# Reordering the queues of a fused attention and gated-unit block: value weights ahead of four tiles of x, fewer filler matmuls

## The chip, the cores and the metric

The kernel runs on one core of a Trainium2 chip (the seven other cores have nothing to do). The metric is the device time of one execution in microseconds, as the median of some runs; lower is better. Four engines compute: TensorE (PE in the profile, with PEld for its weight loads), VectorE (DVE), ScalarE (ACT) and GpSimd (POOL). SyncE (SP) computes nothing; it issues nearly all DMA transfers. Each engine works through its own queue in order and waits on semaphores for what others produce.

## The reference

One layer on x of 2048 rows by 448 columns, in bf16, with 16 heads of 28 columns. Both halves start with a layer norm.

```python
    def _A_ref(x, wqkv, w_phi, wo):
        ...
        pq = jnp.einsum("bhsd,hdf->bhsf", q, w_phi)
        pk = jnp.einsum("bhsd,hdf->bhsf", k, w_phi)
        phi_q = jnp.concatenate([_softmax(pq, axis=-1), _softmax(-pq, axis=-1)], axis=-1)
        phi_k = jnp.concatenate([_softmax(pk, axis=-1), _softmax(-pk, axis=-1)], axis=-1)
        kv = jnp.einsum("bhsf,bhsd->bhfd", phi_k, v)
        z  = jnp.einsum("bhsf->bhf", phi_k)
        num = jnp.einsum("bhqf,bhfd->bhqd", phi_q, kv)
        den = jnp.einsum("bhqf,bhf->bhq", phi_q, z)[..., None] + 1e-6
        o = num / den
        return (lambda x, *d: x.transpose(*d))(o, 0, 2, 1, 3).reshape(B, S, D) @ wo

    def _B_ref(x, w_gate, w_up, w_down):
        g = jnp.einsum("bsd,df->bsf", x, w_gate)
        u = jnp.einsum("bsd,df->bsf", x, w_up)
        h = _sigmoid(g) * u
        return jnp.einsum("bsf,fd->bsd", h, w_down)

    h = x + _A_ref(_layernorm(x, axis=-1), A_wqkv, A_w_phi, A_wo)
    h2 = h + _B_ref(_layernorm(h, axis=-1), B_w_gate, B_w_up, B_w_down)
```

## The kernel before

**Tiles and stages.** The 2048 rows are 16 tiles of 128, numbered 0 to 15. The kernel is one straight program without loops on the chip. Its stages run into each other:

- Front (0 to about 17 us). Weights for keys (ld_k0, ld_k2) and values (ld_v0, ld_v2) and x (x0, x1, x2, x4, ..., the later ones two tiles each, so x6 holds tiles 6 and 7) are loaded. DVE takes the mean and variance of each tile (bst, agg, lines 557 and 558), POOL the inverse root (pow1, line 566), and xn is the normalised tile. Tiles 0 to 3 are transposed on PE (xT0 to xT3, copied out by xT0e to xT3e, lines 550 and 543), tiles 4 to 15 by DMA transposes that SP issues (line 595). The key weights are folded with w_phi on PE (wT, w2m0, copied out by w2e0, line 634), so that the key features come from one product; the query weights likewise (w2m1, w2e1). Filler matmuls on zeros (warm0 to warm9, line 536) stand where PE would have nothing to do.
- Key features (about 10 to 43 us). For tiles 0 to 3, ppa/ppb are the key products of two tiles and vva/vvb the value products; from tile 4 on, pva/pvb do both for one tile. ACT takes the two exponentials of each tile (ek, lines 673 and 674) and copies the values (v1, line 543); DVE sums (ss, line 677) and inverts (rs, line 683); POOL or DVE multiplies (phi, line 687); PE accumulates phi times v into banks 6 and 7 (kva/kvb, line 697), started by a small constant product (seed, line 711). PE squeezes the query products (pqa/pqb, exponentials eq on ACT, line 725) in between.
- Attention output (about 43 to 57 us). The sums in banks 6 and 7 are masked into kvz (kvzA to kvzD, lines 754 and 758). For each tile num is the product with the query features, and DVE does rsm, qq, b, c and rden (lines 802 to 810); o is the normalised output, oT its transpose. The output projection of tiles 0 and 1 (wof0, wof1) includes x, so bs2 and ag2 take the second layer norm's statistics from PSUM, h0 and h1 copy the sum out (lines 834 and 835), hn normalises (line 855), hT0 and hT1 transpose on PE, and hT0e and hT1e copy them out (line 543).
- Gated unit (57 to 199 us). For each of 14 blocks ff of the hidden width, ga and gb are the two halves of the gate and up products: for two tiles at once in the first two groups (ga0_ff, ga2_ff: 256 columns), for four in the rest (512 columns). ACT takes the sigmoid (sig, line 914), DVE or POOL multiplies (hh, line 920). dn and dp are the two halves of the down product, fin adds the residual, out stores.

**What sets the order.** `ORDER` (line 243) lists every operation of each queue by name. The program is traced once, the data dependencies become semaphore waits, and each engine's queue is emitted in that order; an operation that may run on several engines runs on the one whose list has its name.

**Banks.** PSUM has 8 banks. Key products of tile t go to bank t % 2, value products to bank 2 + t % 2, so the product of tile t + 2 waits for ek and v1 of tile t. The query products use banks 0 and 1 or 4 and 5, num for tiles from 2 on uses 6 and 7. In the gated unit an odd ff uses banks 0 and 1, an even ff banks 4 and 5: ga of ff + 2 waits until sig and the reader of the up product of ff are done. In blocks named in `UCOPY` (line 314; 0_2 to 0_13 and all of group 2) ACT copies the up product out (uc, line 919) and the bank is free then; in 0_0 and 0_1 the bank is free only when DVE's hh0_0 and hh0_1 have read it.

**Halves.** Most products run as pairs of 64-row matmuls side by side, which write two banks at once. The a half of an operation writes one bank with the lower rows and the other with the upper rows, the b half the other way round, so the b half must wait until the a half has ended (lines 89 to 102).

The functions that the change and the prediction touch are the lists in `ORDER`, `warm` (lines 533 to 540), `proj2` and `proj`, `ekv`, `kvmask`, `num`, `resid` and `gate_up`.

Of the kernel before, what the change touches and what calls it, by code (L numbers as in the profile page):

```python
# [1042 lines left out]
```

## Time and profile before

| | us |
|---|---|
| Median of 3 runs | 202.06 |
| Lowest and highest run | 201.98 and 202.38 |
| The profiled execution | 201.4 |
| Its span, first to last instruction | 199.5 |
| What lies around the span | 1.9 |

| Engine | busy us | share of the span |
|---|---|---|
| PE, matmuls | 194.7 | 98% |
| PEld, weight loads | 114.3 | 57% |
| DVE | 126.8 | 64% |
| ACT | 100.0 | 50% |
| POOL | 69.5 | 35% |

All times below are microseconds from the start of the span. In rows of the timeline the first number is the start, the second the time until the end of the last of the instructions that the row merges, then engine, line, operation, what it writes and reads, its shape and how many; in square brackets stands how long the engine was idle before it and who released it. In rows of busy time by stretch, each engine's busy time in that stretch is followed by the number of its instructions; then come the granted clock of TensorE, the DMA share and GB/s.

### The profile page before, as it was taken

How to read it: one execution, taken by the hardware profiler on the slowest of the kernel's cores; microseconds unless marked ns; L12 is line 12 of the kernel's file. 1: busy time of each engine (PE TensorE's matmuls, PEld its weight loads, DVE VectorE, ACT ScalarE, POOL GpSimd, SP SyncE). 2: the span in 40 equal slices, each digit the busy share in tenths (PEclk: the TensorE clock that was granted, in tenths of full speed). 3: DMA queues.
4: the chain of work that ended last, by engine and by line, in shares of the span. 5: the costliest groups of instructions: out<-in, count | busy, mean ns of one | idle time of the engine just before them, and what ended most of it. 6: DMA issues, size and time to landing. Idle time of an engine off the chain costs nothing.

```text
span 199.5 us, 5929 instructions
## 1 busy us (share of the span) xinstructions
PE 194.7 (98%) x2528; PEld 114.3 (57%) x2528; DVE 126.8 (64%) x309; ACT 100.0 (50%) x213; POOL 69.5 (35%) x107
## 2 busy tenths in 40 slices
PE   7999999999989999999999999999999999999995
PEld 2835555666557788886555444444555555555553
DVE  6999999978889876286558775246232522353224
ACT  3869899899795776356232443223323212222210
POOL 4689968733543456353303146100210000000000
DMA  6995925478941573213102204203020000003103
GB/s 153 341 128 124 86 56 133 114 228 275 347 60 34 135 114 55 53 37 75 40 17 64 58 3 92 43 0 97 3 53 3 0 0 3 0 0 96 45 3 92
DMA packets 32866, 16.26 MB, mean 82 GB/s; under 512 B 25096, under 2 KB 31944, under 8 KB 32840
## 3 DMA queue, kind: packets, MB, share of 16 engines
q1 hardware_dynamic: 32336, 15.86, 35.3%
q8 instruction: 20, 0.33, 0.7%
q10 hardware_dynamic: 504, 0.03, 0.2%
q14 instruction: 6, 0.05, 0.1%
HBM read 8.34 MB, written 1.84 MB: 51 GB/s over the span
## 4 chain that ended last, share of the span: by engine, by line
PE 92%; DVE 3%; DMA 2%; SPq 1%; issue 1%
PE psum L338 87%; PE psum L960 3%; DMA wk_sb<-in_A_wqkv_dram 2%; PE psum L627 1%; SPq L439 1%; PE psum L536 1%; DVE c_sb L808 1%; DVE st L833 1%; PE psum L550 0%; DVE b_sb L805 0%; DVE hn_pad L855 0%; DVE xnT L543 0%; PE psum L611 0%; DVE x_sb L835 0%; DVE rsm L802 0%
## 5 line engine op out<-in xcount | busy, mean ns | idle before, releaser
L338 PE MATMUL psum<-xnT,wg_sb 64*128 64x512 bf16 (+1 forms) x490 | 95.1, 333 | 0.3 <-DVE xnT L543 0.3
L338 PE MATMUL psum<-xnT,wu_sb 64*128 64x512 bf16 (+1 forms) x490 | 95.0, 333 | 0.1
L914 ACT ACTIVATE sg_sb<-psum 128x512 bf16<-128x512 f32 (+1 forms) x70 | 35.6, 515 | 75.6 <-PE psum L338 75.2
L920 DVE TENSOR_TENSOR hhT<-sg_sb,psum 128x512 bf16<-128x512 bf16 (+1 forms) x44 | 29.2, 674 | 46.6 <-ACT sg_sb L914 46.0
L338 PEld LDWEIGHTS psum<-xnT,wg_sb 64*128 64x128 bf16 x490 | 44.7, 94 | 20.3 <-DVE hhT L920 0.8
L338 PEld LDWEIGHTS psum<-xnT,wu_sb 64*128 64x128 bf16 x490 | 44.6, 94 | 14.0 <-PE psum L338 0.9
L338 PE MATMUL psum<-wd_sb,hhT 64*128 64x448 bf16 x392 | 43.8, 349 | 0.0
L338 PEld LDWEIGHTS psum<-wd_sb,hhT 64*128 64x128 bf16 x392 | 20.9, 94 | 16.8 <-DVE x_sb L840 0.3
L338 PE MATMUL psum<-wv_sb,xnT 64*128 64x448 bf16 x112 | 22.2, 351 | 0.1
L338 PE MATMUL psum<-Wk,xnT 64*128 64x448 bf16 x112 | 22.1, 350 | 0.1
L814 POOL TENSOR_TENSOR o_pad<-c_sb,rden 128x448 bf16<-128x448 bf16 x12 | 11.2, 935 | 26.5 <-DVE rden L810 26.0
L687 POOL TENSOR_TENSOR phi<-hhT,rs 128x896 bf16<-128x896 bf16 x10 | 16.9, 1704 | 2.9 <-DVE rs L683 1.7
L677 DVE TENSOR_REDUCE ss<-hhT 128x32 f32<-128x896 bf16 x16 | 17.0, 1063 | 0.3
L725 ACT ACTIVATE eq<-psum 120x1024 bf16<-120x1024 f32 x16 | 15.8, 1031 | 0.9 <-PE psum L338 0.9
L338 PE MATMUL psum<-xnT,Wq 64*120 64x512 bf16 x112 | 14.8, 384 | 0.1
L967 DVE SCALAR_TENSOR_TENSOR x_sb<-psum,x_sb 128x448 bf16<-128x448 f32 (+2 forms) x17 | 9.7, 594 | 7.5 <-PE psum L338 5.1
L919 ACT CAST xn_pad<-psum 128x256 bf16<-128x256 f32 x26 | 9.4, 375 | 6.4 <-PE psum L338 5.8
L338 PE MATMUL psum<-wo_o,oT 64*128 64x448 bf16 x49 | 11.5, 349 | 0.0
L338 PE MATMUL psum<-wo_e,oT 64*128 64x448 bf16 x49 | 11.5, 349 | 0.0
L920 POOL TENSOR_TENSOR hhT<-sg_sb,xn_pad 128x256 bf16<-128x256 bf16 x11 | 7.6, 694 | 11.1 <-ACT xn_pad L919 6.9
L338 PEld LDWEIGHTS psum<-Wk,xnT 64*128 64x128 bf16 x112 | 7.7, 94 | 5.5 <-PE psum L338 1.0
L805 DVE TENSOR_TENSOR b_sb<-psum,qq 128x464 bf16<-128x464 f32 x16 | 10.1, 634 | 0.7 <-PE psum L338 0.4
(112 smaller groups left out, 244.0 us busy)
## 6 DMA issues: line engine op xcount, KB each, us to landing
out_dram<-x_sb SPq DMA_DIRECT2D x15, 112.0 KB, 1.8
x_sb<-in_A_x_dram SPq DMA_DIRECT2D x7, 224.0 KB, 4.5
wd_sb<-in_B_w_down_dram SPq DMA_DIRECT2D x7, 224.0 KB, 7.5
wg_sb<-in_B_w_gate_dram SPq DMA_DIRECT2D x3, 448.0 KB, 4.5
wu_sb<-in_B_w_up_dram SPq DMA_DIRECT2D x3, 448.0 KB, 4.7
wv_sb<-in_A_wqkv_dram SPq DMA_DIRECT2D x2, 224.0 KB, 4.9
wk_sb<-in_A_wqkv_dram SPq DMA_DIRECT2D x2, 196.0 KB, 3.5
wo_e<-in_A_wo_dram SPq DMA_DIRECT2D x1, 336.0 KB, 3.2
```

The costliest lines, as they stand in the source:

```text
L338: p = e.matmul(o, lhsT=w, rhs=r, start=st, stop=sp, tile_position=(row, 0))
L439: return op(eng, name, lambda e: e.dma_start(dst, src), r=r, w=w, dma="in" if eng == "sp" else "ain", nring=(48 if eng == "sp" else 8) if ...
L677: op("dve", "ss%d" % t, lambda e: e.tensor_reduce(ss[:, s, :].rearrange("p (b h) -> p b h", h=2), eks.rearrange("p b (d h) -> p b h d", h= ...
L687: return e.tensor_tensor(phi[:, sp, :, :, :].rearrange("p b a n -> p (b a) n")[:, :, 0:56].rearrange("p b (d h) -> p b d h", h=2), eks.rea ...
L725: op("act", "eq%d_%d%s" % (c, i, "pm"[sg]), lambda e, sg=sg: e.activation(eq[c][:, sg, 2 * i:2 * i + 2, :].rearrange("p g n -> p (g n)"), ...
L805: op("dve", "b%d" % t, lambda e: e.tensor_tensor(h3(b_sb), OMv[:, :, :, 0:EV], h2(qq)[:, :, :, None].to_broadcast([P, NB, 8, EV]), ALU.mul ...
L814: return e.tensor_tensor(o_pad[:, t % NO, off:off + D].rearrange("p (h d) -> p h d", h=H), c_sb[:, t % NS, :, 0:DH], rden[:, t % NS, :][:, ...
L914: op("act", "sig" + nm, lambda e: e.activation(sg_sb[:, k, 0:N], bk(bg)[:, 0:N], ACT.Sigmoid), r=[B(bg)], w=[("sg", k)])
L919: op("act", "uc" + nm, lambda e: e.copy(up, bk(bu)[:, 0:N]), r=[B(bu)], w=[ub])
L920: op(("pool", "dve") if nm in UCOPY else "dve", "hh" + nm, lambda e: e.tensor_tensor(hhT[(t0 // 4) % NHH][:, ff, ns], sg_sb[:, k, 0:N], up ...
L960: p = e.matmul(bk(b)[:, lo:hi], lhsT=hb[:, ff, TS(t)], rhs=wd_sb[:, ff, lo:hi], start=ff == 0, stop=ff == FT - 1)
L967: op("dve", "fin%d%s" % (t, nm), lambda e: e.scalar_tensor_tensor(out=h_sb[:, t, lo:hi], in0=bk(b)[:, lo:hi], scalar=1.0, in1=h_sb[:, t, l ...
```

## The change

No operation of the layer's mathematics is added or dropped. `ORDER` is written anew for all five queues, and the list of filler matmuls is cut from ten entries (44 matmuls) to six (22). `PACE`, `UCOPY`, `PROGRAM` and `HALF` stay as they are. Some operations change engine: among others xn3, w2e0_3 and nm1_8 go to DVE, xT2e, hT0e, h1 and v1_4 to ACT, v1_12 to DVE, kvzA to ACT and kvzB to DVE, phi0 from DVE to POOL, hn6 and hn7 from DVE to POOL.

```diff
     "sp": (
-        "x1 x0 ld_k0 x2 ld_k2 x4 x6 ld_v0 x10 ld_v2 x8 x12 ld_q1 ld_q2 ld_q0 ld_q3 xT5 xT4 xT6 xT7 x14 xT9 xT8 xT10 "
-        "xT11 xT12 xT13 ld_woe0 xT14 ld_woe1 xT15 ld_woo0 ld_woo1 ld_wg0 ld_wu0 ld_wg1 ld_wu1 ld_wg2 ld_wu2 ld_wg3 "
...
+        "x1 x0 ld_k0 x2 ld_k2 x4 ld_v0 ld_v2 x6 x10 x8 x12 ld_q1 ld_q2 ld_q0 ld_q3 xT4 xT5 x14 xT6 xT7 xT8 xT9 xT11 "
+        "xT10 ld_woe0 xT12 ld_woe1 ld_woo0 xT13 xT14 ld_woo1 xT15 ld_wg0 ld_wu0 ld_wg1 ld_wu1 ld_wg2 ld_wu2 ld_wg3 "
+        "ld_wu3 ld_wd0 oT2 ld_wd1 oT3 oT4 oT5 ld_wd2 oT6 ld_wd3 ld_wd4 oT7 ld_wd5 hT3 ld_wd6 hT2 hT5 hT4 oT9 oT8 hT7 "
...
     "act": (
-        "wphi3 wphi2 wphi1 wphi0 kvzones wTe0 wTe1 xT1e xT0e w2e0_0 w2e0_2 w2e0_3 w2e0_1 nm1_2 xT3e par nm1_6 ek1 ek0 "
-        "v1_0 v1_1 ek2 w2e1_0 nm1_8 v1_2 v1_3 ek3 w2e1_1 ek4 xn10 ek5 v1_5 w2e1_2 w2e1_3 ek6 v1_6 ek7 v1_7 ek8 v1_8 "
-        "eq0_0p ek9 v1_9 ek10 v1_10 eq0_0m ek11 v1_12 ek12 ek13 v1_13 ek14 v1_14 ek15 v1_15 eq0_1m eq0_1p eq1_0p kvzB "
-        "eq1_0m eq1_1p eq1_1m eq2_0p eq2_0m oT0e eq2_1p oT1e eq2_1m h0 eq3_0m eq3_0p eq3_1p eq3_1m sload sig0_1 "
-        "sig0_0 sig0_3 uc0_3 uc0_2 sig0_2 sig0_5 uc0_5 sq2 sig0_4 uc0_4 sq3 sig0_7 uc0_7 uc0_6 sig0_6 sq5 uc0_9 "
...
+        "wphi3 wphi2 wphi1 wphi0 kvzones par wTe1 wTe0 xT1e w2e0_0 xT0e w2e0_2 w2e0_1 xT2e xT3e ek0 ek1 v1_1 "
+        "v1_0 nm1_6 ek2 v1_2 w2e1_0 ek3 v1_3 w2e1_1 ek4 v1_4 w2e1_3 ek5 v1_5 w2e1_2 v1_6 ek6 xn10 nm1_12 ek7 v1_7 ek8 "
+        "v1_8 eq0_0m ek9 v1_9 ek10 v1_10 ek11 v1_11 ek12 eq0_0p ek13 v1_13 ek14 ek15 v1_14 v1_15 eq0_1m eq0_1p eq1_0m "
+        "kvzA eq1_0p eq1_1m eq1_1p eq2_0p eq2_0m oT0e oT1e eq2_1p eq2_1m h1 h0 eq3_0p eq3_0m hT0e eq3_1m eq3_1p "
+        "sig0_1 sload sig0_0 uc0_3 sig0_3 sq2 sig0_2 uc0_2 uc0_5 sig0_5 sq3 sig0_4 uc0_4 uc0_7 sig0_7 uc0_6 sig0_6 "
...
     "pe": (
-        "warm0 wT0 wT1 xT1 warm1 warm2 warm3 xT0 warm4 wT2 wT3 w2m0_0 warm5 w2m0_2 w2m0_1 w2m0_3 warm6 warm7 warm8 "
-        "xT3 ppa0 ppb0 xT2 warm9 vva0 vvb0 ppa2 ppb2 vva2 w2m1_0 vvb2 w2m1_2 w2m1_1 seed pva4 kva1 kvb0 pvb4 pva5 "
-        "kvb1 kva0 pvb5 pva6 w2m1_3 pvb6 kvb2 pva7 kva3 pqa0_0 pvb7 pva8 kvb3 kva2 pvb8 pqb0_0 pva9 kva5 kvb4 pvb9 "
...
-        "kva15 kvb14 pqa1_1 qs pqb1_1 wwo num0 pqa2_0 num1 pqb2_0 num2 pqa2_1 oT0 pqb2_1 pqa3_0 num3 oT1 wof0 wof1 "
-        "num4 pqb3_0 pqa3_1 pqb3_1 hT0 hT1 wgu num5 ga0_1 ga0_0 gb0_1 gb0_0 woa2 num6 ga0_3 ga0_2 gb0_3 wob2 gb0_2 "
-        "ga0_5 num7 gb0_5 ga0_4 gb0_4 ga0_7 woa4 gb0_7 ga0_6 wob4 gb0_6 ga0_9 num8 gb0_9 ga0_8 woa6 gb0_8 wob6 ga0_11 "
...
-        "wob12 gb4_10 ga4_13 gb4_13 ga4_12 dn4_0 gb4_12 dn4_4 ga8_1 ga8_0 gb8_1 gb8_0 dn4_8 dn4_11 ga8_3 ga8_2 dp4_0 "
...
+        "warm0 wT1 wT0 xT0 xT1 w2m0_0 wT2 wT3 xT3 warm1 w2m0_2 w2m0_1 w2m0_3 warm2 warm3 warm4 warm5 xT2 ppa0 ppb0 "
+        "seed vva0 vvb0 ppa2 vva2 ppb2 vvb2 w2m1_0 kva0 w2m1_1 kvb0 pva4 w2m1_2 pvb4 pva5 w2m1_3 pvb5 pva6 kva2 kvb1 "
+        "pvb6 kva1 pva7 pqa0_0 pvb7 pva8 kvb2 kva3 pvb8 pqb0_0 kvb3 pva9 kva4 pvb9 pva10 kvb4 kva5 pvb10 kvb5 pva11 "
...
+        "pvb15 pqa0_1 kva12 kvb11 pqb0_1 kvb13 pqa1_0 kva13 kvb12 pqb1_0 kvb14 kva15 kva14 kvb15 pqa1_1 qs wwo num0 "
+        "pqb1_1 num1 pqa2_0 num2 pqb2_0 pqa2_1 oT0 pqb2_1 num3 oT1 wof0 wof1 num4 pqa3_0 pqb3_0 pqa3_1 num5 hT1 hT0 "
+        "wgu pqb3_1 ga0_1 gb0_1 num6 woa2 ga0_0 ga0_3 gb0_0 gb0_3 wob2 num7 ga0_2 ga0_5 gb0_2 gb0_5 woa4 ga0_4 ga0_7 "
+        "gb0_4 gb0_7 wob4 num8 ga0_6 ga0_9 gb0_6 gb0_9 woa6 ga0_8 ga0_11 gb0_8 gb0_11 wob6 num9 ga0_10 ga0_13 gb0_10 "
...
+        "ga4_6 woa10 gb4_6 ga4_9 wob10 gb4_9 ga4_8 num15 gb4_8 ga4_11 woa12 gb4_11 ga4_10 wob12 gb4_10 ga4_13 dn4_0 "
+        "gb4_13 ga4_12 dn4_4 gb4_12 ga8_1 dn4_8 gb8_1 ga8_0 dn4_11 gb8_0 dp4_0 dp4_4 ga8_3 ga8_2 gb8_3 gb8_2 dp4_8 "
...
     "dve": (
...
+        "zero steps bd0 wopad0 wopad1 mask2 bst1 agg1 bst0 agg0 xn1 xn0 bst3 agg3 bst2 agg2 xn3 wTe2 wTe3 bst5 w2e0_3 "
+        "bst4 agg5 agg4 bst6 bst7 bst11 agg7 bst9 agg6 ss0 agg9 agg11 rs0 bst8 ss1 bst10 rs1 agg10 agg8 xn6 bst12 ss2 "
+        "nm1_8 bst13 rs2 ss3 phi2 ss4 rs3 bst14 bst15 ss5 agg15 agg14 agg12 agg13 ss6 rs5 rs4 xn13 xn12 phi4 rs6 phi5 "
+        "ss7 ss8 rs7 xn14 ss9 rs8 ss10 rs9 rs10 ss11 v1_12 rs11 phi9 ss12 rs12 ss13 ss14 rs13 rs14 phi13 ss15 rs15 "
+        "phi15 kvzC kvzD kvzB rsm0 qq0 b0 c0 rden0 b1 rsm2 c1 qq2 rden1 b2 c2 rden2 rsm3 qq3 b3 c3 bs2_0 rden3 bs2_1 "
+        "rsm4 ag2_1 qq4 ag2_0 b4 c4 hn1 hn0 rsm5 qq5 hT1e rden4 b5 c5 rden5 o5 rsm6 qq6 hh0_1 b6 c6 rden6 hh0_0 h2 "
...
     "pool": (
...
+        "epsl0 v1ones neghalf epsr0 ident0 ident pow1_1 pow1_0 pow1_3 pow1_2 nm1_2 wqpad xn2 pow1_4 nm1_4 phipad xn4 "
+        "xn5 pow1_6 phi0 xn7 phi1 pow1_8 xn8 nb1_8 xn9 xn11 phi3 pow1_12 phi6 xn15 phi7 phi8 phi10 phi11 phi12 phi14 "
...
-        for i, (n, size) in enumerate(((9, 512), (1, 128), (1, 128), (2, 128), (1, 128), (8, 128), (4, 128), (7, 128), (9, 128), (2, 128))):
+        for i, (n, size) in enumerate(((9, 512), (1, 128), (1, 128), (2, 128), (1, 128), (8, 128))):
             op("pe", "warm%d" % i, warm(n, size), r=["zero"], w=[B(3)])
```

For the stretch around 44 to 61 us, DVE's list before the change reads: rs15 phi15 kvzC kvzD kvzA rsm0 qq0 b0 c0 rden0 b1 c1 rsm2 rden1 qq2 b2 c2 rden2 rsm3 qq3 b3 c3 bs2_0 rden3 bs2_1 rsm4 ag2_1 ag2_0 qq4 h1 b4 hn0 hn1 c4 hT0e hT1e rden4 rsm5 qq5 b5 c5 rden5 hh0_1 hh0_0.

75 rows, old and new, of the table ORDER are left out of this document.

## The prediction

> **What bounds the kernel now.** I read the page's busy shares first, then the chain that ended last, then busy time by stretch, then the timelines of the stretches in which another engine is as full as PE.
>
> ```profile
> PE 194.7 (98%) x2528; PEld 114.3 (57%) x2528; DVE 126.8 (64%) x309; ACT 100.0 (50%) x213; POOL 69.5 (35%) x107
> PE 92%; DVE 3%; DMA 2%; SPq 1%; issue 1%
> ...
> 12.40:20.00 7.60, 7.46 (x104) 3.67 (x102) 7.60 (x14) 6.42 (x15) 6.87 (x10) 1.00 0.55 113
> 20.00:30.00 10.00, 10.00 (x172) 5.70 (x166) 9.96 (x23) 9.36 (x20) 8.34 (x6) 1.00 0.64 70
> 30.00:42.10 12.10, 12.10 (x230) 7.49 (x228) 11.64 (x20) 10.55 (x21) 9.56 (x8) 1.00 0.61 154
> 42.10:57.00 14.90, 14.33 (x260) 8.65 (x256) 12.59 (x37) 13.51 (x18) 4.79 (x6) 1.00 0.88 253
> 60.00:197.00 137.00, 136.87 (x1620) 80.20 (x1620) 71.98 (x175) 50.06 (x122) 30.12 (x55) 1.00 0.19 42
> ```
>
> The last five rows give busy time by stretch: stretch, its length, then PE, PEld, DVE, ACT, POOL with their instructions, clock, DMA share, GB/s. PE idles 199.5 - 194.7 = 4.8 us in all, so no order can win much, while a new wait is paid in full: from 60 to 197 us PE is busy for 136.87 of 137.00, so nothing lost before 60 is made up behind it. Before 42.1 PE is not alone. From 12.4 to 42.1 DVE is busy for 7.60 + 9.96 + 11.64 = 29.20 of 29.70 us: the key features are carried by two engines at once. From 42.1 to 57 comes the only real hole, 0.57 us.
>
> **The front: value weights, fillers, value products.** The change takes 22 of 44 fillers out, puts xT2 and xT3 ahead of ppa0, and lets vva0 follow ppb0 with only the seed between.
>
> ```profile
> 9.60 1.74 PE L338 MATMUL psum<-Wk,xnT 64*128 64x448 bf16 x14
> 11.50 0.28 PE L536 MATMUL psum<-zero 128*128 128x128 bf16 x2
> 11.71 1.74 PE L338 MATMUL psum<-wv_sb,xnT 64*128 64x448 bf16 x14
> 13.29 1.74 PE L338 MATMUL psum<-Wk,xnT 64*128 64x448 bf16 x14
> 18.86 0.35 PE L338 MATMUL psum<-wv_sb,xnT 64*128 64x448 bf16 x1
> ...
> 11.38 0.54 ACT L673 ACTIVATE hhT<-psum 128x448 bf16<-128x448 f32 x1 [0.39 <-PE psum L338]
> 12.66 0.56 ACT L674 ACTIVATE hhT<-psum 128x448 bf16<-128x448 f32 x1
> 13.49 0.97 ACT L543 CAST v<-psum 128x448 bf16<-128x448 f32 x2 [0.26 <-PE psum L338]
> ```
>
> The value products vva0 started at 11.71, behind ppb0, xT2 and warm9, and on none of these rows does PE wait for value weights; loading them earlier is worth 0. xT2 and the fillers at 11.50 take the 0.44 us from ppb0's end (9.60 + 1.74 = 11.34) to 11.78, and go. But the next key products, ppa2 at 13.29, write banks 0 and 1 and start when the four exponentials of tiles 0 and 1 end (12.66 + 0.56 = 13.22), and these start when ppb0 ends (11.38). In the new order ppb0 ends no earlier: ppa0 needs all four folded key weights, and w2m0_2 now waits for wTe2, which DVE does behind xn3. I get 9.4 to 9.6 for ppa0 against 9.60. So the 0.44 us fall into a stretch that ACT closes at 13.22: worth 0 here.
>
> Behind that the new PE order is shorter: the seed (0.3) is done, and vva2 between ppa2 and ppb2 saves their drain (0.25, from ppa0, whose 8 matmuls need 0.75 and occupy 1.00 to ppb0 at 10.60). Up to 1.1 us could be there by pva4. However ACT now makes the copies v1_2, w2e1_0, ek3, v1_3, w2e1_1, ek4, v1_4 in one row, and v1_4 came off DVE. At half a microsecond each (0.97 for two casts, 0.54 to 0.56 an exponential, about 0.45 apart), starting when ppb2 ends (about 15.6), v1_3 is done near 18.8, and pva5, which needs its bank, cannot start before; pva5 started at 18.86 before. And DVE carries the stage:
>
> ```profile
> L557 DVE BATCH_NORM_STATS2 st<-x_sb 128x6 f32<-128x448 bf16 x16 | 9.4, 606 | 0.3 <-DMA x_sb<-in_A_x_dram 0.3
> L543 DVE CAST v<-psum 128x448 bf16<-128x448 f32 x2 | 1.2, 592 | 0.0
> L543 DVE COPY xnT<-psum 128x512 bf16<-128x512 bf16 x3 | 1.1, 404 | 0.0
> L543 ACT COPY xnT<-psum 128x512 bf16<-128x512 bf16 x3 | 1.7, 598 | 0.2 <-PE psum L550 0.2
> ```
>
> Counted from 10 us, DVE has two statistics more to do (xn3 and w2e0_3 push them back: 2 x 0.61) and one copy of v (0.59) and xT2e (0.40) less: +0.2 us. Against that stand the 0.5 us that it idled between 12.4 and 42.1. So phi15, which ended that stretch at 42.1, comes between 41.8 and 42.4. **Term 1: 0** (bounds -0.3 and +0.4). Queued loads: x6 goes behind both value loads and lands later by two of them, covered because DVE reaches tile 6 only at 10 us; ld_wd2 to ld_wd6 go behind oT and hT transposes but are read by the down products beyond 71 us; xT12 to xT14 now sit behind loads of the output weights. If that cover is too thin, PE waits for a tile: up to +0.6, kept for the range.
>
> **num0 ahead of pqb1_1.**
>
> ```profile
> 43.20 1.24 DVE L754 TENSOR_TENSOR kvz<-psum,mask 64x232 bf16<-64x232 f32 x3 [1.10 <-PE psum L338]
> 45.47 0.64 DVE L805 TENSOR_TENSOR b_sb<-psum,qq 128x464 bf16<-128x464 f32 x1 [0.42 <-PE psum L338]
> ...
> 44.29 0.84 PE L338 MATMUL psum<-xnT,Wq 64*120 64x512 bf16 x6
> 44.97 0.39 PE L338 MATMUL psum<-kvz,eq 56*128 56x60 bf16 x16
> ```
>
> kvz is ready at 44.44, yet num0's matmuls start at 44.97, behind pqb1_1 (44.29), and DVE stands 0.42 us before b0. With num0 first that wait goes. **Term 2: -0.4** (bounds -0.7, if the masks end sooner too, and -0.1). It is worth something because DVE's chain from b0 to the second layer norm is nearly without holes and decides when the gate products start.
>
> **The entry into the gated unit.** This is the largest term.
>
> ```profile
> 55.21 0.38 PE L338 MATMUL psum<-xnT,Wq 64*120 64x512 bf16 x2
> 56.39 0.40 PE L338 MATMUL psum<-kvz,eq 56*128 56x60 bf16 x16 [0.24 <-DVE c_sb L808]
> 57.06 0.27 PE L338 MATMUL psum<-xnT,wg_sb 64*128 64x256 bf16 x1 [0.26 <-DVE xnT L543]
> 59.92 0.28 PE L338 MATMUL psum<-xnT,wg_sb 64*128 64x256 bf16 x1
> ...
> 54.77 2.85 ACT L725 ACTIVATE eq<-psum 120x1024 bf16<-120x1024 f32 x3
> 57.64 1.28 ACT L897 ACT_TABLE_LOAD   x1
> 58.93 0.20 ACT L897 ACTIVATE sg_sb<-neghalf 128x1 bf16<-128x1 f32 x1
> 59.04 0.64 ACT L914 ACTIVATE sg_sb<-psum 128x256 bf16<-128x256 f32 x2
> ...
> 53.04 0.57 DVE L833 BATCH_NORM_STATS2 st<-psum 128x6 f32<-128x448 f32 x1
> 54.41 0.63 DVE L805 TENSOR_TENSOR b_sb<-psum,qq 128x464 bf16<-128x464 f32 x1
> 54.96 0.74 DVE L855 TENSOR_SCALAR hn_pad<-x_sb,mv,rst 128x512 bf16<-128x512 bf16 x2
> 55.62 0.63 DVE L808 TENSOR_TENSOR c_sb<-b_sb,psum 128x464 bf16<-128x464 bf16 x1
> 56.16 0.75 DVE L543 COPY xnT<-psum 128x512 bf16<-128x512 bf16 x2
> 59.44 0.75 DVE L920 TENSOR_TENSOR hhT<-sg_sb,psum 128x256 bf16<-128x256 bf16 x2 [0.41 <-ACT sg_sb L914]
> ```
>
> Before, pqb3_1 ended at 55.21 + 0.38 = 55.59. Its two exponentials ended at 57.62, the table for the sigmoid was loaded by 58.92, sig0_1 and hh0_1 followed, and hh0_1 (59.44, about 0.42 for one) freed banks 0 and 1 at 59.86 for ga0_3, which started at 59.92. PE filled the time with ga0_1, ga0_0, gb0_1, gb0_0, woa2 and num6.
>
> I put the new order on the old clock, from bs2_1's end at 53.61. DVE does four small ones (0.35), b4 and c4 (1.2), hn1 and hn0 (0.7): hn0 ends at 55.9. Copying h1 went to ACT, which saves DVE 0.5, but b4 and c4 now stand ahead of hn, so the transposes are no earlier. hT0 (0.23 to issue, then its drain) ends at 56.35, hT0e on ACT (0.6, as its copies of such tiles above) at 57.0, and ga0_1 starts at 57.05, as before. But **pqb3_1 now stands behind hT0** in PE's queue: it starts at 56.2 and ends at 57.0, 1.4 us later than before. ACT then needs two exponentials (0.92 + 1.03), the table (1.28) and sig0_1 (0.36), DVE hh0_1 (0.42), with five hand-overs of about 0.03: 57.0 + 4.15 = 61.15. The load itself waits for nothing but ACT's order, so swapping sload with sig0_1 costs nothing. ga0_3 starts at 61.2 instead of 59.92, and gb0_0, three pairs of 0.11 us, is still to do. PE meanwhile has only ga0_1, gb0_1, num6, woa2 and ga0_0, the last of which waits for eq3_1p itself. **Term 3: 61.2 - 59.92 + 0.33 = +1.6** (bounds +0.8, if DVE gets to hn earlier than I count, and +2.0).
>
> On the table, the row says 57.64 + 1.28 = 58.92 and the next activation starts at 58.93. The Trainium skill (ScalarE: Activation LUTs, What ACT_TABLE_LOAD costs) puts about 1.38 us of drain on top of 1.28; by that the entry would be 1.4 us longer in both orders, and the trace does not agree, with 0.01 us behind the load.
>
> **Drains in the gated unit.**
>
> ```profile
> 63.27 0.27 PE L338 MATMUL psum<-xnT,wu_sb 64*128 64x256 bf16 x1
> 63.38 0.61 PE L338 MATMUL psum<-xnT,wu_sb 64*128 64x256 bf16 x2
> 63.72 0.28 PE L338 MATMUL psum<-xnT,wg_sb 64*128 64x256 bf16 x1
> ```
>
> Pairs follow each other by 0.11 us, but from the last pair of ga0_4 (63.38) to gb0_4 (63.72) 0.34 us pass: a b half right behind its a half costs 0.23. Before, ga0_4 and ga4_13 have it so; in the new order only ga0_1, inside the wait of term 3. **Term 4: -0.4** (bounds -0.5 and +0.3, for hh and hn moved to POOL, where hn6 stands behind hh2_8 and hT6 gets some 0.8 us of slack ahead of group 4).
>
> **Sum:** 0 - 0.4 + 1.6 - 0.4 = +0.8 us on the profiled 201.4 (span 199.5 and 1.9 around it): 202.2. The runs' median lies 0.66 higher, at 202.06, so I forecast **202.9**. With the terms' likely spreads it runs from 202.3 to 203.7.
>
> **Rivals.**
>
> - *The front's gain arrives (faster).* Place: pva4 to phi15. If ACT's copies keep up and DVE does its 29 us without holes, 1.1 us pass through to num0; with -0.4 there, -0.5 of drains, and term 3 at 1.3, the sum is -0.7: 201.4. It decides if phi15 ends before about 41.2. Against it: DVE idled only 0.5 us there and has no less to do. Chance 0.12.
> - *The entry costs half.* DVE reaches hn earlier, pqb3_1 ends near 56.2, and term 3 is 0.8; the sum is 0: 202.1. For it: h1 left DVE. Against: b4 and c4 came ahead. Chance 0.19.
> - *Key features come late (slower still).* Features or transposed tiles reach PE late at several kva/kvb and pva, since phi4, phi7 and phi8 are due within 0.1 to 0.2 us of their use by my count: +1.0 more, 203.9. For it: POOL and ACT are 83 to 94% busy from 20 to 30 us. Chance 0.14.
> - *The clock falls.* Fewer fillers leave PE idle in pieces between 5 and 9.5 us. If products ran at half rate for some 3 us from 9.6, the two rows of 1.74 at 9.60 and 11.71 would take some 3 us longer, of which about 1 is hidden: +2 on the forecast, 204.9. Against it: granted clock 1.00 in every stretch. The Trainium skill (TensorE: Matmul & The Clock Gate, What's actually happening) says that an idle window of 3.4 us halves the clock; no such gap is foreseen here. Chance 0.02.
>
> **How the numbers follow.** Forecast 0.53, rivals 0.12, 0.19, 0.14, 0.02. A measurement of this kernel tells about 0.2%, 0.4 us, from no change. The first rival is mostly faster (0.10) and a little within; the second lies mostly within; of the forecast's own spread a tenth reaches into "within". Faster 0.11, same 0.22, slower 0.67. The range leaves out about 0.1 on each side: 201.7 to 204.0; the forecast's own is 202.3 to 203.7.
>
> **What would show it.** In the new profile: ppa2 still starting at the end of the exponentials near 13.2 (front worth nothing); phi15 ending at 42.1 within 0.3; DVE's wait before b0 gone; pqb3_1's matmuls behind the transposes of hn; a PE idle piece of 1.5 us or more ahead of ga0_3, released by DVE's hh or ACT's sigmoid; no 0.23 step at gb0_4 and gb4_13. I am wrong if PE has no such hole near 60 us, or if the key features end a microsecond sooner or later.

## The result, and the profile after

| | kernel before | changed kernel |
|---|---|---|
| Median, us (6 runs each) | 202.02 | 204.88 |
| Lowest and highest | 201.53 and 202.41 | 203.82 and 205.33 |
| Profiled execution and its span | 201.4 and 199.5 | 203.82 and 201.9 |

The changed kernel is slower: ratio 1.0133, 95% interval 1.0102 to 1.0165. The median lies 2.0 us above the forecast of 202.9 and 0.9 us above the range's upper end. The profiled execution is the fastest of its six, so the trace shows a loss of 2.4 us where the medians show 2.9; its other executions left no trace. In five executions of kernels of the next section, one each of entry_old, fetch_moved, pqb_early, pqb_relief and entry_fetch, TensorE's mean granted clock was 0.992 instead of at least 0.998, and each was its kernel's slowest (206.49, 205.52, 206.36, 205.33 and 203.67).

The page of the changed kernel: busy time by engine, the chain that ended last, and the second DMA queue that will matter below (packets, MB, share of 16 engines).

```profile
PE 194.3 (96%) x2506; PEld 109.9 (54%) x2506; DVE 124.0 (61%) x303; ACT 100.8 (50%) x215; POOL 72.0 (36%) x110
...
q8 instruction: 20, 0.33, 0.7%
...
PE 90%; ACT 4%; DMA 2%; DVE 1%; issue 1%; SPq 1%
```

PE does 0.4 us less with 22 matmuls fewer, but the span is 2.4 us longer: idle time went from 4.8 to 7.6 us, and ACT is now on the chain. Busy time by stretch says where. First the kernel before, then the changed one.

```profile
57.00:62.00 5.00, 4.94 (x86) 3.58 (x86) 4.34 (x13) 3.30 (x7) 1.87 (x2) 1.00 0.27 56
62.00:72.00 10.00, 9.93 (x182) 7.47 (x180) 8.73 (x32) 7.67 (x24) 5.07 (x10) 1.00 0.49 113
72.00:197.00 125.00, 124.93 (x1412) 71.24 (x1408) 61.35 (x139) 41.74 (x97) 25.01 (x44) 1.00 0.17 36
```

```profile
42.10:57.00 14.90, 14.65 (x274) 9.12 (x268) 12.81 (x37) 13.08 (x19) 5.11 (x9) 1.00 0.86 238
57.00:62.00 5.00, 3.35 (x58) 1.96 (x56) 3.30 (x9) 4.12 (x6) 0.94 (x1) 1.00 0.41 56
62.00:72.00 10.00, 9.18 (x172) 7.10 (x170) 8.81 (x29) 6.62 (x21) 6.42 (x12) 1.00 0.56 131
72.00:197.00 125.00, 125.00 (x1432) 67.46 (x1427) 57.91 (x136) 43.95 (x102) 27.26 (x46) 1.00 0.17 37
```

Two new holes in PE: 1.65 us between 57 and 62 (0.06 before), and 0.82 us between 62 and 72 (0.07 before). The older hole, 42.1 to 57, shrank from 0.57 to 0.25. The rest of the added idle time, 0.8 us, lies ahead of 12.4, where fillers are gone and the first key product, ppa0, came 0.5 us later. The chain of waits of the changed kernel names what stands behind both (start, length, what; steps of at most 0.05 us are left out):

```profile
55.01 1.94 ACT eq L725 x2
56.94 0.48 ACT xnT L543
...
57.44 1.94 ACT eq L725 x2
...
59.40 1.28 ACT L914
...
60.69 0.39 ACT sg_sb L914
...
61.11 0.43 DVE hhT L920
...
61.59 8.25 PE psum L338 x156
69.84 0.82 issue
```

The first hole is the predicted one: two eq, hT0e and two more eq fill ACT from 55.01 to 59.38, then come the table, sig0_1 and hh0_1, and ga0_3 starts at 61.59 instead of 59.92. The second, 0.82 us at 69.84, is in no term of the forecast. There PE waits for woa6, the output projection of tiles 6 and 7, whose last input is the DMA transposition oT7. In the kernel before, woa6's first weight load started without any wait, and SP had issued oT6 and oT7 directly behind one another, the loads after them (timeline):

```profile
68.24 0.09 PEld L338 LDWEIGHTS psum<-wo_e,oT 64*128 64x128 bf16 x1
...
64.40 2.56 SPq L827 DMA_TRANSPOSE oT<-o_pad  x2
67.01 1.62 SPq L439 DMA_DIRECT2D wd_sb<-in_B_w_down_dram  x3
```

oT7 alone, in the view by tile: how long its issue took (ns), when it was issued, and how long until it landed (us).

```profile
L827 SPq DMA_TRANSPOSE oT<-o_pad x1: 1188/1188/1188, 65.8 to 65.8; - x1
DMA to landing us min/median/max: 2.4/2.4/2.4
```

The same two views of the changed kernel, with ppa0's row and ga0_3's for use below:

```profile
10.11 0.93 PE L338 MATMUL psum<-Wk,xnT 64*128 64x448 bf16 x8
61.59 0.28 PE L338 MATMUL psum<-xnT,wg_sb 64*128 64x256 bf16 x1 [1.42 <-DVE hhT L920]
70.66 0.35 PE L338 MATMUL psum<-wo_e,oT 64*128 64x448 bf16 x1 [0.82 <-issue]
...
65.40 1.08 SPq L439 DMA_DIRECT2D wd_sb<-in_B_w_down_dram  x2
67.16 1.79 SPq L827 DMA_TRANSPOSE oT<-o_pad  x1
```

```profile
L827 SPq DMA_TRANSPOSE oT<-o_pad x1: 1789/1789/1789, 67.2 to 67.2; - x1
DMA to landing us min/median/max: 3.4/3.4/3.4
```

And its DMA queues in the tenth of a microsecond from 67.50 to 67.60:

```profile
q8 instruction: 1, 0.02, 62.2%
```

Before, oT7 landed at 65.8 + 2.4 = 68.2, just as woa6 started: there was no slack. Now oT7 is issued 1.4 us later, since its tile is ready later (in oT7_first below, without the loads ahead of it, it is issued at 67.19 too). PE would reach woa6 at 69.84, 1.6 us later than before, so a landing after 2.4 us would still be in time. But oT7 takes 3.4 us. Two things are new around it: ld_wd3 and ld_wd4 are issued right ahead of it, and a 16 KB block of program code is fetched at 67.5, during its issue. The label of the wait, "issue", means that the profile shows no releaser, so the cause must be found by experiment.

### The profile page after: what moved, and what is told of

The parts are those of the page before. It is cut to its first block, busy times and chain, and to the rows that moved or that the text cites. A ratio compares the mean times of both kernels' runs of the same rounds, so it can differ in the third digit from the quotient of the medians.

```text
span 201.9 us, 5894 instructions
## 1 busy us (share of the span) xinstructions
PE 194.3 (96%) x2506; PEld 109.9 (54%) x2506; DVE 124.0 (61%) x303; ACT 100.8 (50%) x215; POOL 72.0 (36%) x110
## 4 chain that ended last, share of the span: by engine, by line
PE 90%; ACT 4%; DMA 2%; DVE 1%; issue 1%; SPq 1%
PE psum L338 85%; PE psum L960 3%; DMA x_sb<-in_A_x_dram 2%; ACT eq L725 2%; PE psum L627 1%; PE psum L889 1%; PE psum L550 1%; ACT L914 1%; SPq L439 1%; DVE st L557 1%; ACT hhT L673 0%; ACT hhT L674 0%; PE psum L536 0%; ACT xnT L543 0%; DVE hhT L920 0%
## 5 line engine op out<-in xcount | busy, mean ns | idle before, releaser
L338 PEld LDWEIGHTS psum<-wd_sb,hhT 64*128 64x128 bf16 x392 | 19.4, 94 | 17.7 <-DVE x_sb L840 0.3
L814 POOL TENSOR_TENSOR o_pad<-c_sb,rden 128x448 bf16<-128x448 bf16 x13 | 12.2, 937 | 34.1 <-DVE rden L810 34.1
L687 POOL TENSOR_TENSOR phi<-hhT,rs 128x896 bf16<-128x896 bf16 x10 | 17.5, 1758 | 3.6 <-PE psum L338 3.1
L851 POOL TENSOR_TENSOR rst<-ve,neghalf 128x1 f32<-128x1 f32 x14 | 7.8, 565 | 11.2 <-DVE ve L849 10.3
L920 POOL TENSOR_TENSOR hhT<-sg_sb,xn_pad 128x256 bf16<-128x256 bf16 x13 | 8.6, 678 | 8.9 <-ACT xn_pad L919 8.9
L673 ACT ACTIVATE hhT<-psum 128x448 bf16<-128x448 f32 x16 | 8.8, 552 | 3.9 <-PE psum L338 3.7
```

The costliest lines, as they stand in the source:

```text
L338: p = e.matmul(o, lhsT=w, rhs=r, start=st, stop=sp, tile_position=(row, 0))
L673: e.activation(ek[:, s, :, 0, :], src, ACT.Exp)
L687: return e.tensor_tensor(phi[:, sp, :, :, :].rearrange("p b a n -> p (b a) n")[:, :, 0:56].rearrange("p b (d h) -> p b d h", h=2), eks.rea ...
L814: return e.tensor_tensor(o_pad[:, t % NO, off:off + D].rearrange("p (h d) -> p h d", h=H), c_sb[:, t % NS, :, 0:DH], rden[:, t % NS, :][:, ...
L851: op("pool", "pow2_%d" % t, lambda e: e.tensor_tensor(rst2[:, t:t + 1], ve2[:, t:t + 1], neghalf[:, 0:1], ALU.pow), r=[("ve2", t), "neghal ...
L920: op(("pool", "dve") if nm in UCOPY else "dve", "hh" + nm, lambda e: e.tensor_tensor(hhT[(t0 // 4) % NHH][:, ff, ns], sg_sb[:, k, 0:N], up ...
```

## Experiments

All were timed beside the kernel before on the same chip; its median there lay between 201.60 and 201.78. Ratios are to it, with 95% intervals. "Old" and "new" mean the order before and after the change.

**Which part costs.** Four kernels join old and new orders. front_new has the new one up to qs; back_new has it from num0 on; entry_new has it only from num0 to the gate entry (in joining the orders ld_wd4 came behind oT7 in both); entry_old is the changed kernel with the old order there.

```diff
 front_new:  +new order, fillers of the change | old order from num0
 back_new:    old order, fillers of before     | +new order from num0
 entry_new:   old order, fillers of before     | +new: num0 ... gb0_5, oT7, sq2 | old order
 entry_old:  +new order, fillers of the change | old: num0 ... gb0_5, oT7, sq2  | +new order
```

front_new: 

> The new order up to the query sums (qs), the old one from num0 on, in all five queues. Theory (the loss lies behind num0): 202.0 to 202.4, since in the profile of the changed kernel the key features end 0.6 us later but bs2_1 ends at the same 53.6. Rival (the new front is what is slow): 203.0 to 204.5, with PE behind by what the front adds.

back_new: 

> The old order up to the query sums, the new one from num0 on. Theory: 204.0 to 204.9, nearly the whole loss, with PE idle for about 1.4 us ahead of ga0_3 and again ahead of woa6. Rival (the new front is what is slow): 202.0 to 203.0.

entry_new: 

> The kernel before with the new order only between num0 and the entry into the gated unit. Theory: 204.0 to 205.0, hole of 1.4 us ahead of ga0_3 and late oT7. Rival (entry and rest must come together): under 203.0.

entry_old: 

> The changed kernel with the old order only between num0 and the entry into the gated unit (to gb0_5, o7, oT7 and sq2). Theory (the entry costs 2 us and the wait for oT7 follows from it): 201.6 to 202.3. Rival (the wait ahead of woa6 has a cause of its own behind the entry): 202.7 to 203.3.

| kernel | median us | ratio | interval |
|---|---|---|---|
| front_new | 202.35 | 1.0045 | 1.0021 to 1.0069 |
| back_new | 202.75 | 1.0052 | 1.0033 to 1.0071 |
| entry_new | 203.80 | 1.0094 | 1.0078 to 1.0109 |
| entry_old | 202.83 | 1.0047 | 1.0033 to 1.0061 |

The entry alone costs 1.9 us, a little less than expected; with its own neighbours (back_new) the whole back costs only 1.0, far from the expected 204.0 to 204.9, and entry_old, with the old entry, stays at 202.83, in the range of the rival that has a second cause behind the entry. The front costs 0.9 with a wide spread, 201.72 to 204.06. Since the value products never waited for their weights, that was a surprise, and it pointed at something other than the order. (Of entry_old only the times are used here.)

**The wait ahead of woa6.** Five kernels. oT7_first changes SP's queue alone, fetch_moved the number of filler products alone, both_undone does both on the changed kernel; before_fewer and before_more change the number of products in the kernel before, with nearly the same columns in all.

```diff
 oT7_first, both_undone (sp):
-ld_wd2 oT6 ld_wd3 ld_wd4 oT7 ld_wd5
+ld_wd2 oT6 oT7 ld_wd3 ld_wd4 ld_wd5
 fetch_moved, both_undone, before_more (first filler):
-(9, 512)
+(31, 148)
 before_fewer (fillers of the kernel before):
-(9, 512), (1, 128), (1, 128), (2, 128), (1, 128), (8, 128), (4, 128), (7, 128), (9, 128), (2, 128)
+(9, 512), (1, 128), (1, 128), (1, 256), (1, 128), (2, 512), (1, 512), (2, 448), (2, 512), (2, 128)
```

oT7_first: 

> Edit: the changed kernel, on SP's queue oT7 ahead of ld_wd3 and ld_wd4. Two theories for the 1.0 us that the changed kernel loses ahead of woa6 (oT7 issued at 67.16, landed at 70.57, 3.4 us instead of 2.4). Loads theory: the two weight loads issued just before it (ld_wd4 landed at 70.07) hold it back; then oT7 lands 2.4 us after its issue and the time falls by 0.8 to 1.0 us against the changed kernel. Code-fetch theory: the 16 KB block of TensorE's program that was fetched at 67.5, within 0.4 us of the issue, stretched it (its issue took 1.79 us instead of 1.19); then issue and landing stay as they are, and the time falls by less than 0.2 us.

fetch_moved: 

> Edit: the changed kernel, its first warm-up as 31 products of 148 columns instead of 9 of 512 (4,588 columns instead of 4,608), so TensorE's program has as many products as in the kernel before, 22 more, and every later block of code is fetched some 44 instructions, about 1.2 us, earlier. Code-fetch theory: the block now fetched at 67.5 comes at about 66.3, ahead of oT7's issue at 67.2; oT7's issue takes 1.2 us and it lands 2.4 us after, and the time falls by 0.7 to 1.0 us against the changed kernel (oT6 lands later instead, which nothing waits for). Loads theory: ld_wd3 and ld_wd4 still go first, so oT7 still lands after 3.4 us, and the time stays within 0.2 us of the changed kernel.

both_undone: 

> Edit: the changed kernel with both, oT7 ahead of ld_wd3 and ld_wd4, and the first warm-up as 31 products of 148 columns. Theory that the wait ahead of woa6 has two shares, the loads and the code block: oT7's issue takes 1.2 us and it lands 2.4 us after it (67.2 to 69.6), woa6 does not wait, the profile ends 0.9 to 1.0 us ahead of the changed kernel's, and the time is that of the run with the new back (1.005 of the kernel before), where neither stood in the way. If only one of the two counted, the time equals that of the better single edit, 1.006.

before_fewer: 

> Edit: the kernel before, with its warm-up products of 128 columns joined into fewer of up to 512 (9,088 columns become 8,960, 22 products fewer); no order is changed. Code-fetch theory: the block fetched at 63.9 in the kernel before comes about 1.1 us later, at 65.0, inside the issue of oT6 (64.4), whose issue goes from 1.19 to about 2.4 us as in the run with the new front; oT7 queues behind it, woa6 starts 1 us later, and the time grows by 0.4 to 1.0 us against the kernel before. If the new front costs through its order instead (value weights, x tiles, queues), this kernel is within 0.2 us of the kernel before.

before_more: 

> Edit: the kernel before with 22 products more, its first warm-up as 31 products of 148 columns instead of 9 of 512. Code-fetch theory: the block fetched at 63.9 comes about 1.2 us earlier, at 62.7, after oT5 has landed (62.5) and ahead of oT6's issue (64.4); no transposition that TensorE waits for is met, and the time is that of the kernel before within 0.3 us. If any change of the number of products costs (through the clock or the warm-up itself), it is slower by 0.5 us or more, as the kernel with 22 fewer was (1.4 us).

| kernel | median us | ratio | interval |
|---|---|---|---|
| oT7_first | 203.22 | 1.0060 | 1.0045 to 1.0075 |
| fetch_moved | 203.52 | 1.0107 | 1.0075 to 1.0139 |
| both_undone | 202.54 | 1.0041 | 1.0027 to 1.0056 |
| before_fewer | 203.16 | 1.0059 | 1.0042 to 1.0076 |
| before_more | 202.06 | 1.0029 | 1.0009 to 1.0049 |

oT7 by tile in oT7_first, then in fetch_moved, then in both_undone:

```profile
L827 SPq DMA_TRANSPOSE oT<-o_pad x1: 1632/1632/1632, 67.2 to 67.2; - x1
DMA to landing us min/median/max: 2.7/2.7/2.7
```

```profile
L827 SPq DMA_TRANSPOSE oT<-o_pad x1: 1200/1200/1200, 67.4 to 67.4; - x1
DMA to landing us min/median/max: 2.9/2.9/2.9
```

```profile
L827 SPq DMA_TRANSPOSE oT<-o_pad x1: 1190/1190/1190, 67.1 to 67.1; - x1
DMA to landing us min/median/max: 2.4/2.4/2.4
```

Each theory alone missed and both were half right (by its median, 203.52 of 201.78, fetch_moved stands at 1.0086; two executions of 204.77 and 205.52 raise its ratio). Without the loads ahead of it the transposition lands after 2.7 us, with its issue still stretched; without the code block its issue is clean again, yet it lands after 2.9 and was issued 0.3 later, because the block now met ld_wd4. With both undone it takes 2.4, PE has no wait at woa6, and its profile ends 1.0 us ahead of the changed kernel's. In the medians 1.9 us are gained (1.0133 to 1.0041, of 201.7), more than in the profile; the profiled execution of the changed kernel was its best, and whether the wait was longer in the others no trace shows.

before_fewer is the plainest sign that the fillers' number counts: no order is changed, 22 products go, and the kernel loses 1.2 us by the ratio. There it is oT6 that a block meets, at 65.5, and oT7 queues behind it. Its oT6 by tile, the DMA queues from 65.4 to 65.6, and woa6's first product in the timeline:

```profile
L828 SPq DMA_TRANSPOSE oT<-o_pad x1: 2377/2377/2377, 64.9 to 64.9; - x1
DMA to landing us min/median/max: 3.5/3.5/3.5
```

```profile
q8 instruction: 1, 0.02, 43.0%
```

```profile
69.93 0.35 PE L339 MATMUL psum<-wo_e,oT 64*128 64x448 bf16 x1 [0.89 <-issue]
```

By its profile front_new's 0.9 us are of this kind: the block came at 65.0, oT6's issue took 2.44 us from 64.32 on, and woa6 started 1.1 us later than in the kernel before.

before_more has 22 products more and no such wait, but came out 0.2 to 1.0 us slower than the kernel before, where at most 0.3 was expected. So it does not decide against its rival, that any other number of products costs 0.5 us or more, and for the code block speak the traces: a stretched issue and a wait at woa6 in before_fewer and front_new, neither in before_more. Its profile shows only a front 0.6 us later by phi15; why its slower executions, up to 203.76, are slow stays open.

**The entry.** pqb_early moves the key of the forecast's term 3, act_relief takes hT0e and h1 off ACT, pqb_relief does both.

```diff
 pqb_early, pqb_relief (pe):
-num4 pqa3_0 pqb3_0 pqa3_1 num5 hT1 hT0 wgu pqb3_1 ga0_1
+num4 pqa3_0 pqb3_0 pqa3_1 pqb3_1 num5 hT1 hT0 wgu ga0_1
 act_relief, pqb_relief (act, then dve):
-h1 h0 eq3_0p eq3_0m hT0e eq3_1m
+h0 eq3_0p eq3_0m eq3_1m
-rsm4 ag2_1 qq4 ag2_0 b4 c4 hn1 hn0 rsm5 qq5 hT1e rden4
+rsm4 ag2_1 ag2_0 qq4 h1 b4 hn0 hn1 c4 hT0e hT1e rden4 rsm5 qq5
```

pqb_early: 

> Edit: the changed kernel, on TensorE pqb3_1 ahead of num5, hT1 and hT0 instead of behind them. Prediction's theory (pqb3_1 standing behind hT0 is what makes the entry late): the last eq of the group ends about 1 us earlier and the time falls by 1.0 to 1.4 us against the changed kernel. Rival (ScalarE's row is full from 55.0 on: four eq of 0.92 us, and hT0e, now ScalarE's, between the second and the third): hT0 ends 0.86 us later on TensorE, at 57.5, hT0e waits for it, and the third and fourth eq behind hT0e end at about 60.0 instead of 59.4; the hole ahead of ga0_3 grows and the time rises by 0.3 to 0.6 us.

act_relief: 

> Edit: the changed kernel, with h1 and hT0e back on VectorE (in VectorE's order of the kernel before between rsm4 and qq5); TensorE's order stays. Rival theory in its strong form (ScalarE's row alone, full from 55.0 to 59.4, sets the entry): without hT0e's 0.49 us in it the last eq ends 0.5 us earlier and the time falls by 0.4 to 0.6 us against the changed kernel. Two-locks theory (TensorE's pqb3_1, ending at 57.40, and ScalarE's row both end at 59.4): the third and fourth eq now start at 57.42 behind pqb3_1 and end at 59.36; the time stays within 0.2 us of the changed kernel.

pqb_relief: 

> Edit: both at once, the changed kernel with pqb3_1 ahead of num5, hT1 and hT0, and h1 and hT0e on VectorE. Two-locks theory: the four eq follow one another from 55.0 at 0.92 us each and end at 58.8, the table load ends at 60.1, hh0_1 at 60.5, ga0_3 starts at 61.0 instead of 61.6, and the time falls by 0.5 to 0.7 us against the changed kernel; the rest of the entry's loss (1.0 us) stays, since pqb3_0 itself ends at 54.97 instead of 53.81. If pqb3_1's place alone decided, the fall would be 1.0 to 1.4 us; if ScalarE's row alone, this run equals the one with the row relieved.

Measured: 1.0167 (1.0139 to 1.0194), 1.0168 (1.0151 to 1.0185) and 1.0139 (1.0116 to 1.0161), against 1.0133 of the changed kernel. These times hold the wait ahead of woa6 too, and it was not the same: 0.95 us in the profile of pqb_early and 1.75 in that of act_relief, where a block met oT7, against 0.82. The entry by itself, from bs2_1's end to the start of hh0_1, takes 7.48 us in the changed kernel, 8.10 in pqb_early, 8.38 in act_relief and 7.76 in pqb_relief (5.83 in the kernel before). So none of the moves helps there either. PE at woa6 in act_relief, then ACT's rows of pqb_early and of act_relief:

```profile
72.11 0.35 PE L338 MATMUL psum<-wo_e,oT 64*128 64x448 bf16 x1 [1.75 <-issue]
```

```profile
57.40 0.58 ACT L543 COPY xnT<-psum 128x512 bf16<-128x512 bf16 x1 [0.62 <-PE psum L550]
57.88 1.95 ACT L725 ACTIVATE eq<-psum 120x1024 bf16<-120x1024 f32 x2
```

```profile
54.62 1.94 ACT L725 ACTIVATE eq<-psum 120x1024 bf16<-120x1024 f32 x2 [1.19 <-PE psum L338]
57.95 1.94 ACT L725 ACTIVATE eq<-psum 120x1024 bf16<-120x1024 f32 x2 [1.40 <-PE psum L338]
```

In pqb_early ACT waits 0.62 us for the transposition hT0 before hT0e, and the two eq stand behind it in ACT's queue: it is ACT's order that holds. In act_relief ACT idles 1.40 us until pqb3_1 is done: there it is PE's order, and pqb3_1 ended at 57.91 instead of 57.40, because num5 ahead of it waited for VectorE's c4, which the edit had put behind hn1. In pqb_relief both are open, and a third lock shows on DVE:

```profile
57.17 0.76 DVE L543 COPY xnT<-psum 128x512 bf16<-128x512 bf16 x2 [1.07 <-PE psum L550]
...
60.90 0.17 DVE L803 TENSOR_TENSOR qq<-rsm,psum 128x16 f32<-128x16 f32 x1
60.99 0.42 DVE L920 TENSOR_TENSOR hhT<-sg_sb,psum 128x256 bf16<-128x256 bf16 x1
```

sig0_1 was done at 60.07, 1.0 us earlier than in the changed kernel, but hh0_1 stands behind b5, c5, o5, rsm6 and qq6, all of which had moved back behind hT0e's wait of 1.07 us; hh0_1 starts only 0.1 us earlier. In part the edit made this lock: in the changed kernel DVE was through with qq6 at 59.54 and waited 1.56 us for sig0_1. TensorE's granted clock fell in this execution (0.81 in the stretch from 57 to 62), so its products behind 60 us are not compared:

```profile
57.00:62.00 5.00, 3.44 (x47) 1.79 (x46) 4.58 (x14) 3.14 (x5) 0.94 (x1) 0.81 0.15 30
```

So the expected 0.5 to 0.7 us did not come. ACT's order, PE's order and, with these undone, DVE's order each lead to an instant near 61 us; of the kernels here only those with the whole old entry take it back.

**Term 2 and the swaps alone.** num0_only has one swap, swap_only three, both on the kernel before.

```diff
 num0_only, swap_only (pe):
-qs pqb1_1 wwo num0 pqa2_0
+qs wwo num0 pqb1_1 pqa2_0
 swap_only (pe):
-ga0_4 gb0_4 ga0_7
+ga0_4 ga0_7 gb0_4
-ga4_13 gb4_13 ga4_12 dn4_0
+ga4_13 dn4_0 gb4_13 ga4_12
```

num0_only: 

> Edit: the kernel before with num0 ahead of pqb1_1 and nothing else. Prediction's term 2: VectorE's wait ahead of b0 (0.42 us) goes, and 0.4 us are gained. Rival, from the run with three swaps, where b0 came 0.4 us earlier behind phi15 but num3 0.7 us later behind b0: the 0.86 us of pqb1_1 that now stand between num0 and num1 come back at num3, and the time rises by 0.2 to 0.4 us.

swap_only: 

> Edit: the kernel before with three swaps of the change alone, each of which stood as a gain: num0 ahead of pqb1_1, dn4_0 ahead of gb4_13, ga0_7 ahead of gb0_4; warm-ups, queues and entry as before. Theory: the wait ahead of b0 goes (0.4 us) and two drains of 0.23 us go; if all of it arrives, 0.4 to 0.9 us faster than the kernel before. Rival: num0's gain is held up behind oT1 or the transposed tile oT7 ahead of woa6 (in the kernel before it landed at 68.19 and woa6 started at 68.25), and only 0.2 to 0.3 us arrive.

Measured: num0_only 202.04, 1.0020 (1.0008 to 1.0032); swap_only 203.70, 1.0097 (1.0081 to 1.0113). DVE in num0_only:

```profile
45.14 0.19 DVE L776 TENSOR_TENSOR qq<-rsm,psum 128x32 f32<-128x32 f32 x1
45.36 0.64 DVE L806 TENSOR_TENSOR b_sb<-psum,qq 128x464 bf16<-128x464 f32 x1
...
51.24 0.26 DVE L803 RECIPROCAL rsm<-psum 128x16 f32<-128x16 f32 x1 [0.90 <-PE psum L339]
```

The wait ahead of b0 is gone, and stands at rsm3 instead, where DVE waited 0.37 us before and 0.90 now: PE has as much to do until num3 as ever. swap_only, where each swap looked like a gain, loses 2.0 us. In its profile PE waits 1.1 us ahead of dn4_0 for VectorE's h (line 840 of the kernel before), which the old order brings too late for a dn4_0 moved up; the front was 1.2 us late in that execution, and num3 0.3 us later still.

**All undone together.** entry_fetch is entry_old with the first filler as 31 products of 148 columns; fetch_clear has 43 of 107.

```diff
 entry_fetch, fetch_clear (entry_old, first filler):
-(9, 512)
+(31, 148)   in entry_fetch
+(43, 107)   in fetch_clear
```

entry_fetch: 

> Edit: the changed kernel with the old order from num0 to the gate entry (as in entry_old, where oT7 stands ahead of ld_wd4 as well), and the first warm-up as 31 products of 148 columns, so that TensorE's code blocks lie as in the kernel before. Theory that the changed kernel's loss is the entry, the two loads ahead of oT7 and the code fetch: all three are undone, and the time is that of the kernel before within 0.3 us (201.5 to 202.1 where the kernel before shows 201.8), 0.6 to 1.0 us below entry_old. If the new front (value weights ahead of x tiles, value products first) costs anything of its own, it stays at entry_old's 202.6 to 202.9.

fetch_clear: 

> Edit: as entry_fetch (the changed kernel with the old entry), with 43 warm-up products of 107 columns instead of 31 of 148, so that the code block comes another 0.6 us earlier, at about 64.3 instead of 64.9, clear of oT6's issue at 65.0. Code-fetch theory: the executions of entry_fetch at up to 203.7 were those in which the block met oT6; here the median is 201.4 to 201.8, none is above 202.6, and the ratio to the kernel before is 0.998 to 1.000. If those came from something else, the spread stays.

Measured: entry_fetch 201.80, 1.0016 (0.9996 to 1.0035); fetch_clear 202.88, 1.0073 (1.0047 to 1.0099). With the entry, the loads ahead of oT7 and, roughly, the blocks' places undone, nothing of the loss is left that can be told from zero, so the new front and the new order of the gated unit together cost 0.7 us at most. The blocks' places are not quite those of before: in entry_fetch's profile, an execution of 202.56, a block comes at 64.86, oT6's issue at 65.02 takes 1.51 us, and woa6 still waits:

```profile
69.15 0.35 PE L338 MATMUL psum<-wo_e,oT 64*128 64x448 bf16 x1 [0.53 <-issue]
```

fetch_clear, meant to be safer, is a miss. In its profile the block aimed at 64.3 came at 64.94, and woa6 waited 0.54 us as well; and a block at 113.7 met oT12; by tile, and what waited for it on PE:

```profile
L827 SPq DMA_TRANSPOSE oT<-o_pad x1: 1201/1201/1201, 112.6 to 112.6; - x1
DMA to landing us min/median/max: 4.2/4.2/4.2
```

```profile
116.89 0.35 PE L338 MATMUL psum<-wo_e,oT 64*128 64x448 bf16 x1 [1.09 <-DMA oT<-o_pad]
```

A shift of the program moves all 20 blocks, and what one transposition gains another can lose. No kernel here is faster than the kernel before.

## Why the prediction was wrong

The direction was right and the time, 202.9, two microseconds short. What failed is a step outside the four terms. Without it they hold as a sum: both_undone, which keeps every one of them and lacks only the wait ahead of woa6, came out at 1.0041 of the kernel before, +0.8 us (0.5 to 1.1), and +0.8 was the forecast. Its profile agrees from the end of phi15 on: 158.2 us from there, against 157.4 before. In part that is luck, since there term 2 measured -0.6, term 3 +2.0 and term 4, as what is left, about -0.5: misses of either sign that cancel.

The changed kernel's own trace adds up to its +2.4 with two entries more: +0.6 for a later front, -0.6, +2.0, +0.8 for the wait ahead of woa6, and -0.4. That is 1.6 above the sum of the forecast. The other 0.4 of the two microseconds is the distance from the profiled execution to the median, taken over as 0.66 and measured as 1.06.

- **The failed step.** "Queued loads: ... ld_wd2 to ld_wd6 go behind oT and hT transposes but are read by the down products beyond 71 us." This was put at nothing, with up to +0.6 kept in the range for a cover too thin. It asked only when the loads are needed, not what stands behind them in SP's queue: ld_wd3 and ld_wd4 now come right ahead of oT7. And the 22 fillers that go were put at nothing because the time that they free falls into a stretch that ACT closes; that each of them is also two instructions of the program, and so moves every later block of code, was not seen. In their place the runs showed oT7 landing 3.4 us after its issue instead of 2.4, and PE waiting 0.82 us for it. Undoing both was worth 1.0 us in the profile and 1.9 us in the medians. That the transposed tile had no slack (68.2 against 68.24) was in the trace of before.
- **Term 1, front 0: right for the order, 0.6 us out in this trace.** From ppa0 to the end of phi15 it takes 32.5 us before and 32.6 after; ppa2 starts as the exponentials end. But phi15 ended at 42.72, outside the 42.1 within 0.3 that was to show it, since ppa0 itself came 0.5 us later (10.11). Over all 18 profiles ppa0 starts at 9.49 to 10.11 with the new front and at 9.60 to 10.76 with the old one, and phi15 ends at 42.13 to 42.82 and at 42.10 to 43.27. So the new order does not show in it; the profile of the kernel before was among the earliest.
- **Term 2, -0.4: right in size, wrong in nature.** b0 came 0.5 us nearer to phi15, but num0_only shows that the swap by itself loses 0.2 to 0.6 us. By the orders, it paid in the change because pqa3_0 went behind num4 as well, and that made pqb3_0 end at 54.97 instead of 53.81 and filled ACT from 55.0 on; no run has this move alone. Terms 2 and 3 then are two sides of one move.
- **Term 3, +1.6: mechanism half right, size 0.4 short.** Measured +1.67 at ga0_3 and 0.33 for gb0_0, so 2.0, the upper bound; PE's idle piece there was 1.42 us. pqb3_1 ended at 57.40, not 57.0, and all else followed as computed. But "pqb3_1 now stands behind hT0" was only one of the locks: ACT's row was full until 57.42 as well, and undoing pqb3_1's place alone gained nothing.
- **Term 4, -0.4: borne out.** The steps at gb0_4 and gb4_13 are gone, and from ga4_13 to ga8_1 the changed kernel catches up 0.25 us. None of the rivals came: no feature was late, the clock stayed at 1.00, the entry cost more and not half, the front gained nothing. (The price of the clock's rival was counted too high: 3 us at half rate delay the work by 1.5 us, not by 3.)

## What to carry to other kernels

When a queue is reordered, ask of each moved DMA not only when its data is needed but which later transfer now stands behind it, and list the transfers that land with no slack: what delays one of them is paid in full. When several engines end within a few tenths of one another ahead of a wait, undo them together, or the test shows nothing. And a kernel that differs only in its number of instructions is a different kernel: before a gain or loss of half a per cent is put down to an order, run the old order with the new instruction count.
